# Windowed attention and MLP on one core: seven block products for group 1, and the inverse deviation as exp(-ln/2) on ScalarE

## Chip, cores and metric

The kernel runs on one core of one Trainium2 chip. The metric is the device time of one execution in microseconds (us). Before the change the median of three runs is 313.48 us (312.97 to 314.12).

## What is computed

Sliding-window causal attention over 8 batches, 8 heads, 576 positions and head size 64, with a window of 64 keys; its output, laid out as 8 x 576 rows of 512, goes through a normalisation and a two-layer perceptron with a residual.

```python
scores = (1.0 / np.sqrt(D)) * np.matmul(q, k.transpose(0, 1, 3, 2))
rel = pos[:, None] - pos[None, :]
scores = np.where((rel >= 0) & (rel < 64), scores, -1e9)
attn = softmax(scores)                       # over the keys
x = (attn @ v).transpose(0, 2, 1, 3).reshape(B, S, H * D)
mu = mean(x); var = mean((x - mu) ** 2)      # over the 512 columns
xn = (x - mu) / np.sqrt(var + 1e-06) * g_ln
out = x + np.maximum(xn @ w_ch1, 0.0) @ w_ch2   # 512 -> 2048 -> 512
```

## The kernel before

The 4608 rows are cut into nine groups of 512 rows: group g < 8 is the first 512 positions of batch g, and group 8 gathers the last 64 positions of all eight batches (the tails). A group is four blocks of 128 rows (kb 0 to 3). The outer loop runs over the groups. Its pass g, called period g here, runs the perceptron of group g and, between its pieces, the attention of batch g + 1 and the loads, casts and transposes of batch g + 2; tail blocks are done in periods 3, 5 and 7.

The order on every engine is written out by hand. mlp_units gives a list of units, and at(i, f, ...) puts a piece of other work into the slot behind unit i. Engines take their instructions in that order and wait for each other by semaphores.

- First layer: 16 units l1(hc) (line 392), each four matmuls of 512 columns into a PSUM tile hps, followed by a Relu on ScalarE into hrT (line 396). For group 1 the units are l1_half (line 513), 256 tokens of two hidden chunks at a time, so that the first half can start when two blocks of zT are there. The tiles hps, hph, ch, pA and pB come from one pool of two PSUM buffers, ps_mm.
- Second layer: groups 0 and 1 use plain products, l2 (line 404) and l2_two (line 528), each ending in add_out, which scales by rstd (from newton, lines 364 to 381, on VectorE), adds x and stores. Groups 2 to 8 use seven products of half-size blocks (line 464, unit stage(n, p)), with sums of hrT made on VectorE by s_sums (line 443), sums of W2 by w2_sums (line 561), and additions by post (line 471).
- Attention of a block j: s_mm (scores, line 283, and two Exps on ScalarE, line 290), s_mask (VectorE, line 297) and b_step (attn times v, line 317, then on VectorE reciprocal, scaling, and the row statistics mvg, lines 320 to 328).
- z_step makes the normalised rows z. In groups 0 and 1 it only subtracts the mean, on VectorE (line 338), and the factor rstd comes in at add_out. In the other groups POOL computes the factor with a power of -0.5 and then z (lines 342 to 345). A tile rsz holds the small values.
- zt_step brings z into zT: by PE transposes and a copy on ScalarE (lines 357 and 360), or for groups 2 to 7 by a DMA transpose on SP's queue (line 353), except block 3 of groups 3 and 5.
- t_main transposes q and k into qkT, by PE and a copy on ScalarE or VectorE (line 212 or 214), or by a DMA transpose; vB_cur and vB_prev copy pieces of v.

Of the kernel before, what the change touches and what calls it, by code (L numbers as in the profile page):

```python
# [10 lines left out]
FP32 = mybir.dt.float32  # L11
# [4 lines left out]
ALU = mybir.AluOpType  # L16
# [4 lines left out]
def kernel(  # L21
# [44 lines left out]
    gT = p_const.tile([128, NKC], FP32, tag="gT", name="gT")  # L66
    mhalf = p_const.tile([128, 1], FP32, tag="mhalf", name="mhalf")
    w1g = p_const.tile([128, NKC, HID], FP16, tag="w1g", name="w1g")
# [230 lines left out]
    def b_step(g, kb):  # L299
        kblk = f"{g}_{kb}"  # L300
        sfx, nb = ("r", 2) if g == NGRP - 1 else ("", None)
        if kb % 2 == 0:
            if (g, kb // 2) not in x_norm:
                for h in ((1, 0) if g // 2 == 2 else (0, 1)):
                    x_norm[(g, h)] = p_xn.tile([128, 2, DM], FP32, tag="xn" + sfx, name=f"xn_{g}_{h}", bufs=nb)
# [22 lines left out]
        nc.vector.bn_aggr(out=mvg[g][:, kb, :], in_=stats)  # L328
        if g < 2:
            z_step(g, kb)  # L330

    def z_step(g, kb):
        z = p_blk.tile([128, DM], FP16, tag="z", name=f"z_{g}_{kb}")
        zsd[(g, kb)] = z
        xv = x_norm[(g, kb // 2)][:, kb % 2, :]
        mu, var = mvg[g][:, kb, 0:1], mvg[g][:, kb, 1:2]
        if g < 2:
            nc.vector.tensor_scalar(out=z, in0=xv, scalar1=mu, scalar2=None, op0=ALU.subtract)
            return
        t = p_blk.tile([128, 3], FP32, tag="rsz", name=f"rsz_{g}_{kb}")  # L340
        ve, rs, nm = (t[:, i:i + 1] for i in range(3))
        nc.gpsimd.tensor_scalar(out=ve, in0=var, scalar1=1.0, scalar2=EPS, op0=ALU.mult, op1=ALU.add)  # L342
        nc.gpsimd.tensor_tensor(out=rs, in0=ve, in1=mhalf, op=ALU.pow)
        nc.gpsimd.tensor_scalar(out=nm, in0=mu, scalar1=rs, scalar2=-1.0, op0=ALU.mult, op1=ALU.mult)
        nc.gpsimd.tensor_scalar(out=z, in0=xv, scalar1=rs, scalar2=nm, op0=ALU.mult, op1=ALU.add)  # L345

# [36 lines left out]
    def mlp_units(g, split=0, two=False, seven=True):  # L383
# [27 lines left out]
        def add_out(kb):  # L411
            xv = x_norm[(g, kb // 2)][:, kb % 2, :]
            if g < 2:
                nc.vector.scalar_tensor_tensor(
                    out=xv, in0=ch[kb], scalar=rstd[g][:, kb:kb + 1], in1=xv, op0=ALU.mult, op1=ALU.add,
                )
            else:
                nc.vector.tensor_tensor(out=xv, in0=ch[kb], in1=xv, op=ALU.add)
            store(kb)
# [156 lines left out]
    nc.vector.memset(ones1, 1.0)  # L576
    nc.vector.memset(mhalf, -0.5)
    nc.gpsimd.affine_select(
# [87 lines left out]
    for g in range(NGRP):  # L666
        units, s_sums = mlp_units(g, (8, 16)[g] if g < 2 else 0, g == 0, g > 1)
        slots = [[] for _ in range(len(units) + 1)]
# [5 lines left out]
        if g == 0:  # L674
# [13 lines left out]
            at(17, s_mask, 1, 1)  # L688
            at(18, b_step, 1, 0)
            at(21, b_step, 1, 1)  # L690
            at(22, zt_step, 1, 0)
            at(24, zt_step, 1, 1)
            at(26, t_main, 1, 0, 1, 0)
# [10 lines left out]
        if g == 1:  # L704
            at(0, cast_qk, 2, 0)
            at(0, cast_qk, 2, 1)
            at(1, b_step, 1, 3)
            at(2, zt_step, 1, 2)
            at(13, newton, 1, 0, 4)
            at(5, zt_step, 1, 3)  # L710
            at(4, alloc_v, 2)
# [4 lines left out]
            at(4, t_main, 2, 0, 0)  # L716
            at(4, t_main, 2, 1, 0)
            at(6, t_main, 2, 0, 1)
            at(6, t_main, 2, 1, 1)
            at(25, w2_sums, 3, 0, 4)  # L720
            at(28, w2_sums, 3, 4, 8)
            for j in range(4):
                at((9, 13, 16, 19)[j], s_mm, 2, j)
                at((10, 14, 17, 20)[j], s_mask, 2, j)
                at((13, 17, 20, 23)[j], b_step, 2, j)
                at((13, 17, 20, 23)[j], z_step, 2, j)
                at((18, 21, 24, 27)[j], zt_step, 2, j)
# [10 lines left out]
            at(17, make_vB, 3)  # L738
            at(31, s_mm, 3, 0)
            at(31, s_mask, 3, 0)  # L740
            for i, (x, half) in zip((12, 24, 12, 28), ((0, 0), (1, 0), (0, 1), (1, 1))):
                at(i, t_main, 3, x, half, 0)
            at(40, load_qk, 4, 0)
            at(40, load_qk, 4, 1)
            at(40, load_v, 4, 0, 4)
        if g == 2:
            for m, i in enumerate((2, 1, 4)):
                at(4 + 2 * m, w2_sums, i, 0, 4)
                at(5 + 2 * m, w2_sums, i, 4, 8)
        if g > 1 and g + 2 < B:  # L750
# [7 lines left out]
        if g > 1 and b < B:  # L758
            for j in range(4):
# [3 lines left out]
                at((2, 7, 12, 17)[j], b_step, b, j)  # L763
                at((2, 7, 12, 17)[j], z_step, b, j)
                at((12, 12, 18, 23 if b in (3, 5) else 22)[j], zt_step, b, j)
        for n, i in enumerate(TAILS.get(g, ())):
# [3 lines left out]
            at(ts[2], b_step, NGRP - 1, i)  # L770
            at(ts[2], z_step, NGRP - 1, i)
            at(ts[3], zt_step, NGRP - 1, i)
# [34 lines left out]
        for i, u in enumerate(units):  # L807
            if g > 1 and i == 20:
                tbank["shared"] = True
            u()  # L810
            for f, a in slots[i]:
                f(*a)
# [30 lines left out]
```

The softmax here doesn't subtract the row's maximum and nothing guards it: scores larger than these inputs give would overflow.

## Time and profile before

| | |
|---|---|
| median of three runs | 313.48 us |
| the profiled execution | 314.71 us, span from first to last instruction 313.0 us |
| mean granted TensorE clock | 0.999 |
| PE matmul busy | 298.9 us (95%), 3041 matmuls |
| VectorE (DVE) busy | 205.2 us (66%) |
| ScalarE (ACT) busy | 153.4 us (49%), 258 instructions |
| GpSimd (POOL) busy | 166.3 us (53%) |
| chain of waits that ended last | PE 74%, DMA 10%, DVE 7%, SP's queue 4%, POOL 2%, ACT 1% |

A row of the groups of instructions reads: source line, engine, operation, output<-input by the program's names, shapes and count, then busy time in us and mean ns of one, then the idle time of the engine just before them with what ended most of it. A table of stages gives for each stretch of the span its length and the busy time of each engine. In a timeline each row has its start and its duration in us, and in brackets the idle time before it with its releaser. Busy time of a pipelined engine is an upper mark of its work.

### The profile page before, as it was taken

How to read it: one execution, taken by the hardware profiler on the slowest of the kernel's cores; microseconds unless marked ns; L12 is line 12 of the kernel's file. 1: busy time of each engine (PE TensorE's matmuls, PEld its weight loads, DVE VectorE, ACT ScalarE, POOL GpSimd, SP SyncE). 2: the span in 40 equal slices, each digit the busy share in tenths (PEclk: the TensorE clock that was granted, in tenths of full speed). 3: DMA queues.
4: the chain of work that ended last, by engine and by line, in shares of the span. 5: the costliest groups of instructions: out<-in, count | busy, mean ns of one | idle time of the engine just before them, and what ended most of it. 6: DMA issues, size and time to landing. Idle time of an engine off the chain costs nothing.

```text
span 313.0 us, 7473 instructions
## 1 busy us (share of the span) xinstructions
PE 298.9 (95%) x3041; PEld 194.1 (62%) x3041; DVE 205.2 (66%) x385; ACT 153.4 (49%) x258; POOL 166.3 (53%) x251
## 2 busy tenths in 40 slices
PE   6988998899999999999999999999999999999992
PEld 4457544497554468646964686459646855784582
DVE  1689585855674996589666965896669636751642
ACT  1496633477416752776247526762475058306500
POOL 7578666454760798369814983698145506200000
PEclk9999999999999999999999999999999999999999
DMA  8999999998866996798179997993690393003013
GB/s 192 267 390 290 320 336 272 280 304 184 159 144 196 268 206 105 243 312 147 37 212 316 203 149 219 316 142 67 209 172 19 62 209 117 2 2 134 0 36 101
DMA packets 109892, 57.42 MB, mean 183 GB/s; under 512 B 79841, under 2 KB 100833, under 8 KB 109858
## 3 DMA queue, kind: packets, MB, share of 16 engines
q1 hardware_dynamic: 108944, 54.02, 69.1%
q0 software_dynamic: 768, 2.80, 3.7%
q8 instruction: 24, 0.39, 0.5%
q10 hardware_dynamic: 146, 0.13, 0.1%
q14 instruction: 10, 0.08, 0.1%
HBM read 38.80 MB, written 9.44 MB: 154 GB/s over the span
## 4 chain that ended last, share of the span: by engine, by line
PE 74%; DMA 10%; DVE 7%; SPq 4%; POOL 2%; ACT 1%; issue 1%; POOLq 0%; ACTq 0%
PE hps L392 30%; PE pA L464 11%; PE pC L464 7%; PE pB L464 7%; PE ch L404 6%; DMA w2s<-in_moe_w_ch_dram 4%; DMA qk<-in_k_dram 4%; PE xps L317 3%; PE sc L283 3%; PE hph L513 3%; PE tp L226 2%; SPq L141 2%; DVE sS L443 2%; DMA w1s<-in_moe_w_ch_dram 2%; SPq L89 1%; DVE pt L297 1%
## 5 line engine op out<-in xcount | busy, mean ns | idle before, releaser
L392 PE MATMUL hps<-zT,w1g 128*128 128x512 f16 x480 | 110.4, 379 | 0.0
L396 ACT ACTIVATE hrT<-hps 128x512 f16<-128x512 f32 x120 | 71.9, 599 | 50.7 <-PE hps L392 47.2
L392 PEld LDWEIGHTS <-w1g 128*128 128x128 f16 x480 | 44.6, 98 | 49.3 <-issue 1.0
L290 ACT ACTIVATE pt<-sc 128x512 f16<-128x512 f32 x72 | 39.0, 595 | 29.8 <-DVE xn L471 15.6
L464 PEld LDWEIGHTS <-sS 128*128 128x128 f16 x448 | 43.3, 98 | 5.1
L342 POOL TENSOR_SCALAR rsz<-mvg 128x1 f32<-128x1 f32 x28 | 10.7, 382 | 60.4 <-DVE mvg L328 59.8
L128 POOL CAST qk<-qk 128x1024 f16<-128x1024 f32 x32 | 35.1, 1112 | 13.4 <-DMA qk<-in_q_dram 6.9
L464 PEld LDWEIGHTS <-hrT 128*128 128x128 f16 x336 | 32.6, 98 | 5.2
L212 ACT COPY qkT<-tp 128x1024 f16<-128x1024 f16 x16 | 16.1, 1012 | 35.2 <-PE tp L226 26.1
L297 DVE TENSOR_TENSOR pt<-pt,mask 128x1024 f16<-128x1024 f16 x32 | 25.4, 800 | 11.9 <-ACT pt L290 11.9
L471 DVE TENSOR_TENSOR xn<-pA,xn 128x512 f32<-128x512 f32 x28 | 19.2, 686 | 21.1 <-PE pA L464 21.1
L443 DVE TENSOR_TENSOR sS<-hrT 128x512 f16<-128x512 f16 (+1 forms) x42 | 24.8, 591 | 10.2 <-ACT hrT L396 10.2
L464 PE MATMUL pA<-wT,sS 128*128 128x256 f16 x224 | 26.9, 273 | 0.0
L345 POOL TENSOR_SCALAR z<-xn,rsz 128x512 f16<-128x512 f32 x28 | 25.3, 902 | 2.9
L464 PE MATMUL pC<-w2s,sS 128*128 128x256 f16 x224 | 26.8, 273 | 0.0
L325 DVE BATCH_NORM_STATS2 stats<-xn 128x6 f32<-128x512 f32 x36 | 25.0, 695 | 1.2
L323 DVE TENSOR_TENSOR xn<-xps,rcp 128x512 f32<-128x512 f32 x36 | 24.9, 692 | 1.2
L513 PE MATMUL hph<-zT,w1g 128*128 128x256 f16 x192 | 23.2, 272 | 2.3 <-ACT zT L360 1.1
L320 DVE RECIPROCAL rcp<-xps 128x8 f32<-128x8 f32 x36 | 7.4, 205 | 26.8 <-PE xps L317 26.8
L404 PE MATMUL ch<-w2s,hrT 128*128 128x512 f16 x96 | 23.1, 380 | 0.0
L513 PEld LDWEIGHTS <-w1g 128*128 128x128 f16 x192 | 18.3, 98 | 5.1 <-issue 2.6
L317 PEld LDWEIGHTS <-pt 128*64 128x64 f16 x576 | 12.2, 110 | 14.4 <-issue 6.4
(85 smaller groups left out, 395.1 us busy)
## 6 DMA issues: line engine op xcount, KB each, us to landing
out_dram<-xn SPq DMA_DIRECT2D x34, 256.0 KB, 2.6
qk<-in_q_dram SPq DMA_DIRECT2D x16, 512.0 KB, 6.2
qk<-in_k_dram SPq DMA_DIRECT2D x16, 512.0 KB, 7.4
v<-in_v_dram SPq DMA_DIRECT2D x32, 256.0 KB, 6.5
w2s<-in_moe_w_ch_dram SPq DMA_DIRECT2D x12, 512.0 KB, 5.7
w1s<-in_moe_w_ch_dram SPq DMA_DIRECT2D x4, 512.0 KB, 6.7
tk<-in_k_dram SPq DMA_DIRECT2D x8, 256.0 KB, 4.7
tv<-in_v_dram SPq DMA_DIRECT2D x8, 256.0 KB, 5.3
```

The source lines that it names most:

```text
L128: nc.gpsimd.tensor_copy(out=dst[:, :].rearrange("p (a j) e d -> p a e j d", j=j), in_=t[:, :].rearrange("p (a e j d) -> p a e j d", e=2, j ...
L290: nc.scalar.activation(out=o, in_=i, func=AF.Exp, bias=0.0, scale=scale)
L297: nc.vector.tensor_tensor(out=ptv, in0=ptv, in1=mb, op=ALU.mult)
L323: nc.vector.tensor_tensor(out=xn, in0=xps[:, :, 0:D], in1=rcp_b, op=ALU.mult)
L325: nc.vector.bn_stats(out=stats, in_=xv)
L345: nc.gpsimd.tensor_scalar(out=z, in0=xv, scalar1=rs, scalar2=nm, op0=ALU.mult, op1=ALU.add)
L392: nc.tensor.matmul(out=hps, lhsT=w1g[:, kc, 128 * hc:128 * (hc + 1)], rhs=zT[g][:, kc, :], start=(kc == 0), stop=(kc == NKC - 1),)
L396: nc.scalar.activation(out=hrT[:, hc, :], in_=hps, func=AF.Relu, bias=0.0, scale=1.0)
L404: nc.tensor.matmul(out=ch[kb], lhsT=hrT[:, hc, 128 * kb:128 * (kb + 1)], rhs=w2s[:, hc, :], start=(hc == 0), stop=(hc == NHC - 1),)
L443: nc.vector.tensor_tensor(out=o, in0=x, in1=y, op=op)
L464: nc.tensor.matmul(out=bank[which][:, p, :], lhsT=a[:, c, 128 * p:128 * p + 128], rhs=wv[:, c, :], start=(first and p == 0 and c == 0), st ...
L513: nc.tensor.matmul(out=hps[:, e], lhsT=w1g[:, kc, 128 * hc:128 * (hc + 1)], rhs=zT[g][:, kc, 256 * half:256 * half + 256], start=(kc == 0) ...
```

## The change

Group 1 joins the groups that use seven block products. For this its z must already be scaled, so newton, its rstd and the scaled add_out are left to group 0. In z_step the power on POOL is replaced, for all groups but 0, by two activations on ScalarE: lv = Ln(var + eps) and rs = Exp(-0.5 lv). z = (x - mu) * rs follows in one instruction, on VectorE for group 1 and on POOL for the others. z_step now stands three slots behind b_step in most places (two or three in periods 0 and 1). The sums of W2 move from periods 1 and 2 to the end of period 0 and the start of period 1; sums of hrT are added for group 1 in period 1. In period 1 the copies of k's transposes of batch 2 go to ScalarE (last argument 0 of t_main). Some slots of batch 3's transposes and scores move by two or three, and the tiles x_norm of groups 3, 4 and 7 are taken in reversed order (before: groups 4 and 5).

```diff
@@ -64,7 +64,7 @@
     mbias = p_const.tile([128, 64], FP16, tag="mbias", name="mbias")
     magt = p_const.tile([128, 4], FP32, tag="magt", name="magt")
     gT = p_const.tile([128, NKC], FP32, tag="gT", name="gT")
-    mhalf = p_const.tile([128, 1], FP32, tag="mhalf", name="mhalf")
+    epst = p_const.tile([128, 1], FP32, tag="epst", name="epst")
     w1g = p_const.tile([128, NKC, HID], FP16, tag="w1g", name="w1g")
     w2s = p_const.tile([128, NHC, DM], FP16, tag="w2s", name="w2s")
     w2v = w2s[:, :, :].rearrange("p (c e) (f d) -> p c e f d", e=2, f=2)
@@ -301,7 +301,7 @@
         sfx, nb = ("r", 2) if g == NGRP - 1 else ("", None)
         if kb % 2 == 0:
             if (g, kb // 2) not in x_norm:
-                for h in ((1, 0) if g // 2 == 2 else (0, 1)):
+                for h in ((1, 0) if g in (3, 4, 7) else (0, 1)):
                     x_norm[(g, h)] = p_xn.tile([128, 2, DM], FP32, tag="xn" + sfx, name=f"xn_{g}_{h}", bufs=nb)
         xv = x_norm[(g, kb // 2)][:, kb % 2, :]
         xn = xv.rearrange("p (h d) -> p h d", h=H)
@@ -326,7 +326,7 @@
         if g not in mvg:
             mvg[g] = p_grp.tile([128, 4, 2], FP32, tag="mvg" + sfx, name=f"mvg_{g}", bufs=1 if sfx else 2)
         nc.vector.bn_aggr(out=mvg[g][:, kb, :], in_=stats)
-        if g < 2:
+        if g == 0:
             z_step(g, kb)
 
     def z_step(g, kb):
@@ -334,15 +334,15 @@
         zsd[(g, kb)] = z
         xv = x_norm[(g, kb // 2)][:, kb % 2, :]
         mu, var = mvg[g][:, kb, 0:1], mvg[g][:, kb, 1:2]
-        if g < 2:
+        if g == 0:
             nc.vector.tensor_scalar(out=z, in0=xv, scalar1=mu, scalar2=None, op0=ALU.subtract)
             return
-        t = p_blk.tile([128, 3], FP32, tag="rsz", name=f"rsz_{g}_{kb}")
-        ve, rs, nm = (t[:, i:i + 1] for i in range(3))
-        nc.gpsimd.tensor_scalar(out=ve, in0=var, scalar1=1.0, scalar2=EPS, op0=ALU.mult, op1=ALU.add)
-        nc.gpsimd.tensor_tensor(out=rs, in0=ve, in1=mhalf, op=ALU.pow)
-        nc.gpsimd.tensor_scalar(out=nm, in0=mu, scalar1=rs, scalar2=-1.0, op0=ALU.mult, op1=ALU.mult)
-        nc.gpsimd.tensor_scalar(out=z, in0=xv, scalar1=rs, scalar2=nm, op0=ALU.mult, op1=ALU.add)
+        t = p_blk.tile([128, 2], FP32, tag="rsz", name=f"rsz_{g}_{kb}")
+        lv, rs = t[:, 0:1], t[:, 1:2]
+        nc.scalar.activation(out=lv, in_=var, func=AF.Ln, bias=epst[:, 0:1], scale=1.0)
+        nc.scalar.activation(out=rs, in_=lv, func=AF.Exp, bias=0.0, scale=-0.5)
+        eng = nc.vector if g == 1 else nc.gpsimd
+        eng.tensor_scalar(out=z, in0=xv, scalar1=mu, scalar2=rs, op0=ALU.subtract, op1=ALU.mult)
 
     def zt_step(g, kb, eng="act"):
         z = zsd.pop((g, kb))
@@ -410,7 +410,7 @@
 
         def add_out(kb):
             xv = x_norm[(g, kb // 2)][:, kb % 2, :]
-            if g < 2:
+            if g == 0:
                 nc.vector.scalar_tensor_tensor(
                     out=xv, in0=ch[kb], scalar=rstd[g][:, kb:kb + 1], in1=xv, op0=ALU.mult, op1=ALU.add,
                 )
@@ -574,7 +574,7 @@
     nc.vector.memset(mask, 1.0)
     nc.vector.memset(magt, RSQRT_MAGIC)
     nc.vector.memset(ones1, 1.0)
-    nc.vector.memset(mhalf, -0.5)
+    nc.vector.memset(epst, EPS)
     nc.gpsimd.affine_select(
         out=mask[0:64], in_=mask[0:64], compare_op=ALU.is_gt, fill=0.0,
         base=0, channel_multiplier=1, pattern=[[-1, 64]],
@@ -664,7 +664,7 @@
 
     TAILS = {3: [0], 5: [1], 7: [2, 3]}
     for g in range(NGRP):
-        units, s_sums = mlp_units(g, (8, 16)[g] if g < 2 else 0, g == 0, g > 1)
+        units, s_sums = mlp_units(g, (8, 16)[g] if g < 2 else 0, g == 0, g > 0)
         slots = [[] for _ in range(len(units) + 1)]
 
         def at(i, f, *a):
@@ -687,9 +687,14 @@
             at(17, s_mm, 1, 1)
             at(17, s_mask, 1, 1)
             at(18, b_step, 1, 0)
+            at(20, z_step, 1, 0)
             at(21, b_step, 1, 1)
-            at(22, zt_step, 1, 0)
-            at(24, zt_step, 1, 1)
+            at(23, z_step, 1, 1)
+            at(23, zt_step, 1, 0)
+            at(26, zt_step, 1, 1)
+            for m, i in enumerate((3, 2, 4)):
+                at(25 + 2 * m, w2_sums, i, 0, 4)
+                at(26 + 2 * m, w2_sums, i, 4, 8)
             at(26, t_main, 1, 0, 1, 0)
             at(27, t_main, 1, 1, 1, 1)
             at(28, vB_cur, 1, 2, 0)
@@ -703,27 +708,31 @@
             at(31, b_step, 1, 2)
         if g == 1:
             at(0, cast_qk, 2, 0)
-            at(0, cast_qk, 2, 1)
+            at(2, cast_qk, 2, 1)
             at(1, b_step, 1, 3)
-            at(2, zt_step, 1, 2)
-            at(13, newton, 1, 0, 4)
-            at(5, zt_step, 1, 3)
+            at(1, z_step, 1, 2)
+            at(4, z_step, 1, 3)
+            at(2, w2_sums, 1, 0, 4)
+            at(3, w2_sums, 1, 4, 8)
+            at(3, zt_step, 1, 2)
+            at(7, zt_step, 1, 3)
+            for i in range(1, 5):
+                at((12, 12, 13, 14)[i - 1], s_sums, 0, 4, i)
+                at((16, 16, 18, 20)[i - 1], s_sums, 4, 8, i)
             at(4, alloc_v, 2)
             at(4, alloc_qkT, 2)
             at(4, alloc_vB, 2)
             at(5, cast_v, 2, 0, 4)
             at(5, make_vB, 2)
             at(4, t_main, 2, 0, 0)
-            at(4, t_main, 2, 1, 0)
+            at(4, t_main, 2, 1, 0, 0)
             at(6, t_main, 2, 0, 1)
-            at(6, t_main, 2, 1, 1)
-            at(25, w2_sums, 3, 0, 4)
-            at(28, w2_sums, 3, 4, 8)
+            at(6, t_main, 2, 1, 1, 0)
             for j in range(4):
                 at((9, 13, 16, 19)[j], s_mm, 2, j)
                 at((10, 14, 17, 20)[j], s_mask, 2, j)
                 at((13, 17, 20, 23)[j], b_step, 2, j)
-                at((13, 17, 20, 23)[j], z_step, 2, j)
+                at((15, 19, 22, 25)[j], z_step, 2, j)
                 at((18, 21, 24, 27)[j], zt_step, 2, j)
             at(3, load_qk, 3, 0)
             at(4, load_qk, 3, 1)
@@ -736,17 +745,13 @@
             at(14, cast_v, 3, 2, 4)
             at(17, alloc_vB, 3)
             at(17, make_vB, 3)
-            at(31, s_mm, 3, 0)
-            at(31, s_mask, 3, 0)
-            for i, (x, half) in zip((12, 24, 12, 28), ((0, 0), (1, 0), (0, 1), (1, 1))):
+            at(28, s_mm, 3, 0)
+            at(29, s_mask, 3, 0)
+            for i, (x, half) in zip((12, 22, 12, 25), ((0, 0), (1, 0), (0, 1), (1, 1))):
                 at(i, t_main, 3, x, half, 0)
             at(40, load_qk, 4, 0)
             at(40, load_qk, 4, 1)
             at(40, load_v, 4, 0, 4)
-        if g == 2:
-            for m, i in enumerate((2, 1, 4)):
-                at(4 + 2 * m, w2_sums, i, 0, 4)
-                at(5 + 2 * m, w2_sums, i, 4, 8)
         if g > 1 and g + 2 < B:
             at(11, alloc_qkT, g + 2)
             if g + 2 >= XQ:
@@ -761,14 +766,14 @@
                     at((2, 7, 12)[j - 1], s_mm, b, j)
                     at((3, 8, 13)[j - 1], s_mask, b, j)
                 at((2, 7, 12, 17)[j], b_step, b, j)
-                at((2, 7, 12, 17)[j], z_step, b, j)
+                at((5, 10, 15, 20)[j], z_step, b, j)
                 at((12, 12, 18, 23 if b in (3, 5) else 22)[j], zt_step, b, j)
         for n, i in enumerate(TAILS.get(g, ())):
             ts = (10, 11, 14, 20) if n else (1, 2, 5, 11)
             at(ts[0], s_mm, NGRP - 1, i)
             at(ts[1], s_mask, NGRP - 1, i)
             at(ts[2], b_step, NGRP - 1, i)
-            at(ts[2], z_step, NGRP - 1, i)
+            at(ts[2] + 3, z_step, NGRP - 1, i)
             at(ts[3], zt_step, NGRP - 1, i)
         n = g + 2
         if g > 1 and n < B:
@@ -805,7 +810,7 @@
             at(7, t_tail, TAILS[g][1], 0)
             at(8, t_tail, TAILS[g][1], 1)
         for i, u in enumerate(units):
-            if g > 1 and i == 20:
+            if g > 0 and i == 20:
                 tbank["shared"] = True
             u()
             for f, a in slots[i]:
```

## The prediction

> **What bounds the kernel now.** I read the page's busy shares first, then the groups of instructions, then a table of stages cut at the borders of period 2, then ScalarE's timeline there.
>
> ```profile
> PE 298.9 (95%) x3041; PEld 194.1 (62%) x3041; DVE 205.2 (66%) x385; ACT 153.4 (49%) x258; POOL 166.3 (53%) x251
> ...
> L392 PE MATMUL hps<-zT,w1g 128*128 128x512 f16 x480 | 110.4, 379 | 0.0
> L396 ACT ACTIVATE hrT<-hps 128x512 f16<-128x512 f32 x120 | 71.9, 599 | 50.7 <-PE hps L392 47.2
> ...
> L342 POOL TENSOR_SCALAR rsz<-mvg 128x1 f32<-128x1 f32 x28 | 10.7, 382 | 60.4 <-DVE mvg L328 59.8
> ```
>
> TensorE (PE) is busy in 95% of the span. ScalarE's Relus wait for PE and never the reverse (the hps row has no idle time), and POOL's small operations wait for their input, so POOL has time to spare.
>
> ```profile
> 96.40:112.80 16.40, 16.40 (x169) 7.93 (x162) 13.80 (x27) 12.93 (x23) 9.27 (x11) 1.00 0.95 240
> 112.80:128.50 15.70, 15.30 (x177) 13.04 (x175) 12.20 (x21) 4.77 (x7) 13.71 (x21) 1.00 0.93 156
> ```
>
> Columns: stretch, length, then busy time of PE, PEld, DVE, ACT, POOL. The first stretch is the first layer of period 2, the second its second layer. ScalarE's 49% hides two things: it is busy 12.9 of 16.4 us in the first layer, and 4.8 of 15.7 us in the second. The first-layer stages are where an addition to ScalarE meets a limit.
>
> ```profile
> 103.56 0.60 ACT L396 ACTIVATE hrT<-hps 128x512 f16<-128x512 f32 x1 [0.27 <-PE hps L392]
> 104.42 0.60 ACT L396 ACTIVATE hrT<-hps 128x512 f16<-128x512 f32 x1 [0.27 <-PE hps L392]
> 105.13 1.08 ACT L290 ACTIVATE pt<-sc 128x512 f16<-128x512 f32 x2
> 106.11 0.60 ACT L396 ACTIVATE hrT<-hps 128x512 f16<-128x512 f32 x1
> ```
>
> A unit of PE takes 0.86 us, its Relu 0.60; ScalarE idles 0.27 per unit, and at an attention step (b_step and s_mm, 0.73 on PE; two Exps, 1.0 on ScalarE) not at all. The hps tiles have two PSUM buffers, so PE can be only two units ahead.
>
> ```profile
> 1.35 1.28 ACT L212 ACT_TABLE_LOAD   x1 [1.35 <-PEq L827]
> ```
>
> That is the only activation table load of the whole kernel.
>
> **What the Trainium skill says.** "ScalarE: Activation LUTs", section "What ACT_TABLE_LOAD costs": a switch of the table set is an instruction on ScalarE of about 1283 ns, plus about 1380 ns of drain. The trace has 1.28 us for the load; 5.37 us of waiting for PE follow it, so no drain can be seen or excluded. Section "Table sets: the hidden batching unit": Relu and copy are in every set, and one set holds both exp and ln. The program as built does not use that one throughout: it has 65 loads where the one before has 1, one ahead of every Ln and one ahead of every Exp of z_step. The Relus and attention's Exps need no more. "TensorE: Matmul & The Clock Gate", "Part 1": PE falls to half clock after an idle window of about 3.4 us; the trace shows 1.00 granted in both stretches above, with PE never idle that long.
>
> **The change, part by part.**
>
> (1) *Inverse deviation on ScalarE.* All blocks but group 0's (32) drop three POOL operations (about 0.54, 0.55 and 0.26 us in the timeline; POOL is not on the path: gain 0 on PE) and put on ScalarE's queue: load, Ln, load, Exp. The trace has no 128x1 activation; the skill's section above prices 280 ns with a pointer bias, 186 ns with an immediate, plus 0.83 ns an element. By the same formula 128x512 is 613 ns; the trace has 599, near enough. So T = 1.28 + 0.28 + 1.28 + 0.19 = 3.03 us, with dispatch **T = 3.1** (estimate). Bounds: below, 0.47 if neither load costs anything; above, 3.1 + 2 x 1.38 = 5.8 with the drains. I take 3.1: the built program issues no drain of its own. The first load also waits for mvg (DVE); z_step was moved three slots behind b_step, so in first layers mvg is there (101.5 for a block due at 103.3).
>
> What is queued behind: the next Relus. Step it at slot 5 of period 2. Let Relu 5 end at 0. Units 6 and 7 end at 0.92 on PE, then slot 7's attention step, 1.65. Unit 8 needs Relu 6, which now ends at T + 0.60: it starts at T + 0.67 = 3.77, 2.1 us late. Then Relu 7 and two Exps precede Relu 8, which ends at T + 2.8; unit 10 could start at T + 2.4: 0.5 more. About 0.1 of that is lost without the block. So **T - 0.6 = 2.5 us of PE per block in a first layer**. PE regains nothing later, since it had no idle time to give.
>
> Which blocks fall there, by ScalarE's order in the changed program: two each in periods 2, 4 and 6, three in 3 and 5 (a tail block too), one in 7: 13 x 2.5 = **32.5**.
>
> (2) *Second layers of periods 2 to 7.* ScalarE has about 11 us free there, so kb 2's block (3.1) is covered. kb 3's mvg comes at 119.4 in period 2; the block ends at 122.5, then the waiting qkT copy (1.0) and POOL's z (0.9): 123.5, where PE wants to transpose z at 121.9: 1.7 late, in periods 2 and 4. In 3, 5 and 6 z goes by a DMA transpose (median 3.0 us to landing): period 3's z would be ready at 155.7, its zT at 158.7, with the next first layer at 160.1: covered by 1.4; I allow 1.0 in all for its queue. In period 7 the tail's mvg is at 269.85, z at 273.9, PE's transpose at 273.1: 0.8. Sum **5.2**.
>
> (3) *Period 0.* Before, DVE needs nobody for z. Now z_0 waits for ScalarE and stands in DVE's queue ahead of b_step (1,1) and of add_out(0): mvg 44.5, z_0 at 47.7 instead of 44.6, second mvg 50.1 instead of 47.4, add_out(0) done at 50.9 instead of 49.2, which frees the PSUM bank of ch_2; then z_1 at 53.3 and ztp of kb 1 at 53.9 (49.0 before, but now due two units later). Behind it DVE has the six W2 sums (0.66 each, up to 1.29 for two), a qkT copy (1.23) and the masks of the last two score blocks. Following DVE's order, add_out(3) ends near 65.5 instead of 62.3, and period 1's third unit waits for that bank: **+3.1**.
>
> (4) *Period 1, first layer.* Blocks kb 2 and 3 stand between its Relus, and two qkT copies (1.0 each) move from DVE to ScalarE. Stepped: third Relu 69.9 (63.5 + 6.4), fifth 71.8, second block to 74.9, two copies to 76.9, Relu 5 and 6 to 78.1, two copies to 80.1, Relu 7, zT copy to 81.3. The second half of the tokens starts at 81.4 against 69.85: 11.5, of which **8.4** are new. SP and POOL's moved cast (slot 0 to 2) have landed data and free time: 0.
>
> (5) *Period 1, rest.* Seven products replace 64 matmuls of 512 columns (3.45 us per 16) by 112 of 256 (1.75 per 16): 13.8 - 12.25 = 1.5 gained on PE. newton's 0.6 us wait goes. The eight sums of hrT (0.69 each) on DVE replace newton (3.0) and two copies (2.5): 0. Against that, four blocks of 3.1, two pairs of Exps and two copies (2.0), 17 us, stand in a stage of 16: the sc buffers, a masked block and the second qkT transpose wait about 2.0 together, and kb 3's rs comes at the very end, so that z (0.9) and its DMA transpose (3.0) reach zT about 3.3 late. Net 5.3 - 2.1 = **+3.2**. Bounds: -2.1 and +8.
>
> The eight W2 sums leave periods 1 and 2, where DVE has time: 0. x_norm's tiles of three groups are taken in another order because group 1 now stores rows 256 to 511 first: the tile asked for first is the one freed first, 0; covered by the stores' 2.6 us to landing.
>
> Sum: 32.5 + 5.2 + 3.1 + 8.4 + 3.2 = **52.4 us**. The profiled execution took 314.71 (span 313.0); the median of the three runs is 313.48, 1.2 below. So 367.1 against its own time, **366** against the median. Each 0.1 us in T is worth about 2.5 us (13 first-layer blocks, about 4 in later second layers, 8 in the serial chains of periods 0 and 1).
>
> **Rivals.**
> A. *Each load drains* (T = 5.8): 2.7 x 25 = 68 more, **433**, and PE's gaps would pass 3.4 us, so the clock could fall too. For it: the skill's figure. Against: no drain is among the instructions. One drain per pair gives 400. Chance 0.12.
> B. *The stalls overlap more than I step*: blocks in periods 0 and 1 run in slack that my chain denies, and half of the first-layer stalls fall in PE's own waits: about half of the sum, **340**. The absence of idle time on PE speaks against. Chance 0.09.
> C. *The loads are no real switch* (no time for them, because exp and ln lie in one set): T = 0.47, below the 0.6 that the two buffers cover. Only the 1.5 and 0.6 of (5) remain, less latency in period 0: **312**. It decides from T under 0.6. Against: the built program loads anew at every turn, and one load showed 1.28 us. Chance 0.04.
> D. My forecast, 350 to 380: chance 0.75.
>
> **How the numbers follow.** About 0.5% (1.6 us) is what a measurement of this kernel can tell from no change. A, B and D lie far above that; C splits 0.03 faster, 0.01 within. The range 345 to 400 leaves out the upper part of A (0.09) and the lower parts of B and C (0.09).
>
> **What would show it.** Right: 65 ACT_TABLE_LOADs, ScalarE's busy time up by some 95 us to near 250; in the first layers PE waiting for "ACT hrT L396" twice a period for about 2 us, where no such wait stands now; first-layer stages of some 21.4 us in place of 16.4, and second layers near 16; POOL's L342 to L344 rows gone. Wrong: one load only (C), gaps of over 1 us after each load (A), PE still over 90% busy, or a span under 345.

## The result and the profile after

The changed kernel takes 378.98 us in the median of four runs (375.49 to 381.11), the kernel before 313.62 us on the same chip (four runs, 312.97 to 314.12). The ratio is 1.2075, 95% interval 1.1976 to 1.2173. The profiled execution took 379.96 us, its span is 378.2 us (before 313.0), and the mean granted clock is 0.954 (before 0.999).

From the page of the kernel after, the busy shares and then rows of the groups of instructions:

```profile
PE 319.5 (84%) x3089; PEld 205.4 (54%) x3089; DVE 212.9 (56%) x383; ACT 247.6 (65%) x388; POOL 156.9 (41%) x167
...
L392 PE MATMUL hps<-zT,w1g 128*128 128x512 f16 x480 | 119.5, 398 | 23.2 <-ACT hrT L396 19.3
...
L345 POOL TENSOR_SCALAR z<-xn,mvg,rsz 128x512 f16<-128x512 f32 x28 | 58.2, 2078 | 138.8 <-ACT rsz L343 84.1
...
L342 ACT ACT_TABLE_LOAD x32 | 41.1, 1283 | 7.9 <-DVE mvg L328 7.5
...
L343 ACT ACT_TABLE_LOAD x32 | 41.1, 1283 | 0.6
```

PE is busy in 84% of its span instead of 95%. The hps row had no idle time; now it has 23.2 us, 19.3 of them behind ScalarE's Relu. There are 64 table loads of 1.283 us in z_step, 82.2 us together. One row changed that the prediction gave no weight to: POOL's z takes 2078 ns in the mean.

ScalarE's timeline in period 2, at the place where a block stands between two Relus:

```profile
118.72 0.60 ACT L396 ACTIVATE hrT<-hps 128x512 f16<-128x512 f32 x1 [0.27 <-PE hps L392]
119.33 1.28 ACT L342 ACT_TABLE_LOAD   x1
120.62 0.29 ACT L342 ACTIVATE rsz<-mvg,epst 128x1 f32<-128x1 f32 x1
120.94 1.28 ACT L343 ACT_TABLE_LOAD   x1
122.23 0.20 ACT L343 ACTIVATE rsz<-rsz 128x1 f32<-128x1 f32 x1
122.34 1.06 ACT L396 ACTIVATE hrT<-hps 128x512 f16<-128x512 f32 x2
```

From the first load's start to the end of Exp it is 3.10 us, and no idle time lies between the five instructions. The table of stages for period 2 (stretch, length, then busy time of PE, PEld, DVE, ACT and POOL, PEclk, DMA share, GB/s):

```profile
110.80:133.00 22.20, 18.36 (x160) 8.48 (x161) 10.41 (x20) 17.34 (x29) 5.21 (x4) 0.92 1.00 226
133.00:153.10 20.10, 17.03 (x177) 13.87 (x176) 11.80 (x21) 10.67 (x15) 13.93 (x16) 0.92 0.35 82
```

The first layer takes 22.2 us instead of 16.4, the second 20.1 instead of 15.7. Both have a granted clock of 0.92. PE's longest waits (what it waited for, us in total, times, longest):

```profile
PE hps L392 <- ACT hrT L396: 19.3, 11, 2.6
PE ztp L357 <- POOL z L345: 6.8, 3, 2.3
PE hps L392 <- DMA zT<-z: 3.4, 2, 2.7
```

The first is what the prediction named. The second is where it was short. The third it had forecast at the border of period 2, where zT was to be about 3.3 us late; the wait there is 2.74 us.

### The profile page after: what moved, and what is told of

Its sections match the earlier page's. It is cut to its first block, busy times and chain, and to the rows that moved or that the text cites. A ratio compares the mean times of both kernels' runs of the same rounds, so it can differ in the third digit from the quotient of the medians.

```text
span 378.2 us, 7630 instructions
## 1 busy us (share of the span) xinstructions
PE 319.5 (84%) x3089; PEld 205.4 (54%) x3089; DVE 212.9 (56%) x383; ACT 247.6 (65%) x388; POOL 156.9 (41%) x167
## 4 chain that ended last, share of the span: by engine, by line
PE 28%; ACT 20%; DVE 13%; issue 12%; DMA 11%; POOL 7%; SPq 5%; POOLq 1%; ACTq 0%; DVEq 0%
PE hps L392 14%; ACT L342 6%; DVE sS L443 5%; ACT L343 4%; PE pA L464 4%; DMA qk<-in_q_dram 3%; POOL z L345 3%; ACT hrT L396 3%; SPq L141 3%; PE pC L464 2%; PE pB L464 2%; PE hph L513 2%; DMA vB<-vA 2%; ACT pt L290 2%; DVE pt L297 2%
## 5 line engine op out<-in xcount | busy, mean ns | idle before, releaser
L392 PE MATMUL hps<-zT,w1g 128*128 128x512 f16 x480 | 119.5, 398 | 23.2 <-ACT hrT L396 19.3
L345 POOL TENSOR_SCALAR z<-xn,mvg,rsz 128x512 f16<-128x512 f32 x28 | 58.2, 2078 | 138.8 <-ACT rsz L343 84.1
L392 PEld LDWEIGHTS <-w1g 128*128 128x128 f16 x480 | 47.0, 101 | 78.7 <-issue 34.4
L464 PEld LDWEIGHTS <-sS 128*128 128x128 f16 x512 | 51.0, 101 | 7.5
L342 ACT ACT_TABLE_LOAD x32 | 41.1, 1283 | 7.9 <-DVE mvg L328 7.5
L464 PEld LDWEIGHTS <-hrT 128*128 128x128 f16 x384 | 38.0, 100 | 6.9 <-issue 0.5
L343 ACT ACT_TABLE_LOAD x32 | 41.1, 1283 | 0.6
L471 DVE TENSOR_TENSOR xn<-pA,xn 128x512 f32<-128x512 f32 x32 | 21.9, 685 | 34.1 <-PE pA L464 34.1
L443 DVE TENSOR_TENSOR sS<-hrT 128x512 f16<-128x512 f16 (+1 forms) x46 | 29.8, 647 | 12.7 <-ACT hrT L396 11.7
L464 PE MATMUL pA<-wT,sS 128*128 128x256 f16 x256 | 33.9, 289 | 0.1
L464 PE MATMUL pC<-w2s,sS 128*128 128x256 f16 x256 | 31.5, 276 | 0.0
L513 PEld LDWEIGHTS <-w1g 128*128 128x128 f16 x192 | 19.4, 104 | 7.1 <-issue 3.6
L518 ACT ACTIVATE hrT<-hph 128x512 f16<-128x512 f32 x24 | 14.2, 600 | 12.2 <-PE hph L513 12.1
```

The costliest lines, as they stand in the source:

```text
L342: nc.scalar.activation(out=lv, in_=var, func=AF.Ln, bias=epst[:, 0:1], scale=1.0)
L343: nc.scalar.activation(out=rs, in_=lv, func=AF.Exp, bias=0.0, scale=-0.5)
L345: eng.tensor_scalar(out=z, in0=xv, scalar1=mu, scalar2=rs, op0=ALU.subtract, op1=ALU.mult)
L392: nc.tensor.matmul(out=hps, lhsT=w1g[:, kc, 128 * hc:128 * (hc + 1)], rhs=zT[g][:, kc, :], start=(kc == 0), stop=(kc == NKC - 1),)
L443: nc.vector.tensor_tensor(out=o, in0=x, in1=y, op=op)
L464: nc.tensor.matmul(out=bank[which][:, p, :], lhsT=a[:, c, 128 * p:128 * p + 128], rhs=wv[:, c, :], start=(first and p == 0 and c == 0), st ...
```

## Experiments

The kernels are shown in one table: how much later than before period 2 starts (terms 3 to 5 of the sum), and by how much the six first layers (term 1) and the six second layers (term 2) of periods 2 to 7 are longer than before, read on PE in the one profiled execution of each, in us, to about 0.1. The ratio is that of all timed runs to the kernel before on the same chip. e3's profiled execution was its lowest run (323.62), e10's its highest (324.03). e9 has one run, 317.45 us, and serves for durations on POOL only.

| kernel | start of period 2 | first layers | second layers | median | ratio (95%) |
|---|---|---|---|---|---|
| forecast | +14.7 | +32.5 | +5.2 | 366 | |
| after | +14.4 | +34.6 | +16.3 | 378.98 | 1.2075 (1.1976 to 1.2173) |
| e1 one load in all | +8.5 | +5.2 | +3.6 | 330.35 | 1.0532 (1.0493 to 1.0570) |
| e2 POOL's old form of z | +10.5 | +31.6 | +3.9 | 361.49 | 1.1551 (1.1502 to 1.1601) |
| e3 both | +5.8 | +3.7 | -0.8 | 327.50 | 1.0406 (1.0366 to 1.0446) |
| e8 e3, loads in first layers | +7.4 | +34.2 | -0.8 | 355.15 | 1.1299 (1.1264 to 1.1335) |
| e4 power on POOL again | +13.1 | +0.1 | -0.9 | 327.80 | 1.0462 (1.0422 to 1.0502) |
| e6 after, more matmuls | +14.4 | +34.4 | +14.7 | 378.02 | 1.2063 (1.2023 to 1.2102) |
| e10 e3, slots moved | +5.9 | +3.7 | -0.3 | 322.40 | 1.0262 (1.0231 to 1.0293) |
| e11 e10 without the sums | -0.4 | +3.7 | -0.7 | 317.54 | 1.0127 (1.0099 to 1.0155) |
| e5 inverse deviation alone | -0.9 | +3.7 | +0.1 | 317.84 | 1.0136 (1.0109 to 1.0162) |
| e7 the same with the loads | +1.4 | +32.2 | +3.4 | 350.42 | 1.1173 (1.1134 to 1.1212) |
| e12 e5, tails two slots later | -1.8 | +0.2 | +1.1 | 315.76 | 1.0049 (1.0030 to 1.0069) |

### What the loads cost: e1, e7 and e5, e8

e1 puts one load of the set that holds Ln, Exp and Relu ahead of everything, after which the program has no other:

```diff
+    nc.scalar.add_instruction(mybir.InstLoadActFuncSet(
+        name=nc.get_next_instruction_name(), ins=[], outs=[], act_func_set_id=6))
     load_qk(0, 0)
```

> The changed kernel with one line ahead of everything: an explicit load of the table set that holds exp, ln, relu and copy. All 64 later loads fall away; Ln, Exp and their order stay. Theory 1 (the loads are nearly the whole cost): each block on ScalarE shrinks from 3.10 us to about 0.5, below the 0.6 that two PSUM buffers cover; 310 to 314 us, no waits of PE for hrT in first layers. Theory 2 (a large part comes from z on POOL, 2.07 us now against 0.8 before, and from the slots that moved): it stays well above the kernel before, 320 to 330. Theory 3 (the clock falls in PE's gaps): the gaps go with the loads, so it cannot be told from theory 1 here; granted clock back at 0.99 or more.

It takes 330.35 us, 48.6 less than after. ScalarE's timeline in period 2 of e1:

```profile
112.56 0.60 ACT L396 ACTIVATE hrT<-hps 128x512 f16<-128x512 f32 x1 [0.27 <-PE hps L392]
113.06 0.29 ACT L342 ACTIVATE rsz<-mvg,epst 128x1 f32<-128x1 f32 x1
113.37 0.20 ACT L343 ACTIVATE rsz<-rsz 128x1 f32<-128x1 f32 x1
113.48 0.58 ACT L396 ACTIVATE hrT<-hps 128x512 f16<-128x512 f32 x1
```

The block is now 0.5 us long and PE does not wait for it. So one set does serve all three functions, as the Trainium skill says ("ScalarE: Activation LUTs", "Table sets: the hidden batching unit"); the program as built only did not use it. Yet 330 us is not the 312 of rival C: something else costs 17 us.

The pair e5 and e7 is the kernel before with Ln and Exp for groups 2 to 8 and the later z slots, group 1 as it was; e5 has the one load, e7 has 57.

```diff
-        nc.gpsimd.tensor_scalar(out=ve, in0=var, scalar1=1.0, scalar2=EPS, op0=ALU.mult, op1=ALU.add)
-        nc.gpsimd.tensor_tensor(out=rs, in0=ve, in1=mhalf, op=ALU.pow)
+        nc.scalar.activation(out=lv, in_=var, func=AF.Ln, bias=epst[:, 0:1], scale=1.0)
+        nc.scalar.activation(out=rs, in_=lv, func=AF.Exp, bias=0.0, scale=-0.5)
...
-                at((2, 7, 12, 17)[j], z_step, b, j)
+                at((5, 10, 15, 20)[j], z_step, b, j)
...
-            at(ts[2], z_step, NGRP - 1, i)
+            at(ts[2] + 3, z_step, NGRP - 1, i)
```

> The kernel before with only the inverse deviation changed: Ln and Exp on ScalarE for groups 2 to 8, z_step two or three slots later as in the change, one table set loaded at the start, POOL's z in its old form; group 1 keeps plain products and newton. If what the changed kernel loses besides loads and form lies in periods 0 and 1 (period 1's VectorE), only the tail blocks' later z is left, 1.8 us each in periods 3 and 5: 315 to 318. If moving the power off POOL gains anything: under 313.

> The same, without the explicit load, so that 56 table loads come in ahead of Ln and Exp: the loads' price on the otherwise unchanged kernel. By the rule of 2.5 us for each of 13 blocks in first layers, 1 to 2 us in second layers of periods 2 and 4, 1 in 7, and some 2 in period 1: 38 to 42 us more than without them, 353 to 359.

The 56 further loads cost 32.6 us, less than the 38 to 42 expected, and most of it in the first layers (+32.2 against +3.7). e8 shows that it is the loads there and not the place of the functions: e3 with two loads of the same set put back into the 13 blocks that the prediction counted.

```diff
+        first = (3 <= g <= 7 and kb < 2) or (g == NGRP - 1 and kb < 3)
+        if first:
+            nc.scalar.add_instruction(mybir.InstLoadActFuncSet(
+                name=nc.get_next_instruction_name(), ins=[], outs=[], act_func_set_id=6))
         nc.scalar.activation(out=lv, in_=var, func=AF.Ln, ...)
...
```

> As the run with one set and POOL's old form, but with two table loads (of the same set again) put back into just the 13 blocks that stand between the Relus of a first layer in periods 2 to 7. The rule of the prediction, T - 0.6 a block with T = 3.1, gives 13 x 2.5 = 32.5 us more than without them. If a block's cost is really spread over later waits: under 26 more; if it also delays what follows: 36 or more.

27.7 us more by the medians, 30.5 in the first layers of the profiled executions: 2.1 to 2.35 us per block, where the prediction had 2.5. Part of this is not the block itself but a lowered clock (see e6).

### POOL's form of z: e2, e3, e9

The change also rewrote z on POOL, from x*rs + nm to (x - mu)*rs. The trace's view of that tile, first after, then before (minimum, median and maximum in ns):

```profile
L345 POOL TENSOR_SCALAR z<-xn,mvg,rsz x28: 2059/2072/2266, 93.8 to 334.5; 128x512 f16<-128x512 f32 x28
```

```profile
L345 POOL TENSOR_SCALAR z<-xn,rsz x28: 762/795/1611, 80.6 to 271.5; 128x512 f16<-128x512 f32 x28
```

e2 is the kernel after with the old form; e3 is e2 with e1's single load.

```diff
-        eng.tensor_scalar(out=z, in0=xv, scalar1=mu, scalar2=rs, op0=ALU.subtract, op1=ALU.mult)
+        if g == 1:
+            nc.vector.tensor_scalar(out=z, in0=xv, scalar1=mu, scalar2=rs, op0=ALU.subtract, op1=ALU.mult)
+            return
...
+        nc.gpsimd.tensor_scalar(out=nm, in0=mu, scalar1=rs, scalar2=-1.0, op0=ALU.mult, op1=ALU.mult)
+        nc.gpsimd.tensor_scalar(out=z, in0=xv, scalar1=rs, scalar2=nm, op0=ALU.mult, op1=ALU.add)
```

> The changed kernel, loads and all, but POOL makes z in its old form, x * rs + (-mu * rs), with one small product ahead, instead of (x - mu) * rs. Theory 1: no more than 2 us less than the changed kernel. Theory 2: z is ready about 1.0 us earlier (2.07 against 0.3 + 0.8), which shortens PE's waits for z in the second layers of periods 2, 4 and 7 and for zT at the borders: 3 to 8 us less, 371 to 376. Theory 3: as theory 2, plus fewer second layers at a lowered clock.

> One table set loaded at the start, and POOL's z in its old form: both suspects gone, the seven products, W2 sums and moved slots of the change stay. If loads and form add up in separate places, the run with one set (330.3) loses about 9 us of its second layers in periods 2 to 7, which then last as before: 319 to 323. If they share one wait, 326 or more. If all the rest of the change costs nothing: 312 to 314.

With the loads in place the old form saves 17.5 us, where 3 to 8 were expected; 12.4 of them are in the second layers (+3.9 instead of +16.3), and some of those are the clock's (below). Without the loads it saves 2.9 (330.35 to 327.5). So the slow form is dear only where z is late already.

e9 is the kernel before with four forms of z, one for each kb, seven instructions each: kb 0 (x - mu)*rs, kb 1 (x + (-mu))*rs, kb 2 x*rs - mu*rs, kb 3 x*rs + (-mu*rs).

> The kernel before, with POOL's z made in four forms by block: kb 0 (x - mu) * rs, kb 1 (x + (-mu)) * rs, kb 2 x * rs - mu * rs, kb 3 as before x * rs + (-mu * rs). If the order of the operations (multiply, then add) is what is fast: kb 0 and 1 at 2.0 us and kb 2 and 3 at 0.8. If only the pair multiply-add has a fast path: kb 3 alone at 0.8. If subtract is slow: kb 0 and 2 at 2.0. If it is contention and not the form: all alike.

Its groups of instructions on POOL (lines 345, 348, 351, 354 are kb 0 to 3; busy us, mean ns, idle before):

```profile
L345 POOL TENSOR_SCALAR z<-xn,mvg,rsz 128x512 f16<-128x512 f32 x7 | 15.7, 2236 | 0.8
L351 POOL TENSOR_SCALAR z<-xn,rsz 128x512 f16<-128x512 f32 x7 | 15.3, 2193 | 0.7
...
L348 POOL TENSOR_SCALAR z<-xn,rsz 128x512 f16<-128x512 f32 x7 | 9.3, 1322 | 0.7
...
L354 POOL TENSOR_SCALAR z<-xn,rsz 128x512 f16<-128x512 f32 x7 | 5.9, 840 | 0.8 <-DMA zT<-z 0.2
```

The two forms with a subtraction never took less than 2077 ns; both with additions went down to 762 to 767 ns. It is the subtraction, in either place, and not the order of the two steps. Why is not shown. Additions were at times slow as well (up to 2127 ns), so a single duration on POOL does not tell the form.

### Does the lowered clock cost something: e6

In the kernel after, units 7 and 12 of the first layers of periods 2 to 6 do their matmuls three times, 17 us of work for PE where it waits.

```diff
-            for kc in range(NKC):
+            for kc in list(range(NKC)) * (3 if 2 <= g <= 6 and hc in (7, 12) else 1):
```

> The changed kernel with the matmuls of first-layer units 7 and 12 made three times over in periods 2 to 6 (same tile, the last pass counts): 1.7 us of PE work in front of the place where PE waits 1.85 to 2.6 us for ScalarE, twice a period, 17 us of added matmul work in all. Theory 1: the added work hides in the waits, and the time stays within 3 us of the changed kernel. Theory 3: the gaps no longer let the clock fall in first layers, granted clock 0.97 to 0.98, and 4 to 10 us less. If the waits were not real: 17 us more.

The time is 378.02 us against 378.98: within the 3 us of the first theory, without the 4 to 10 us of the third. PE's wait for hrT falls to the second line of this list of waits, and the mean clock rises from 0.954 to 0.973:

```profile
PE ztp L357 <- POOL z L345: 8.1, 5, 2.3
PE hps L392 <- ACT hrT L396: 5.1, 2, 2.6
```

Seventeen us of PE's work cost nothing in all: most of them fit into PE's waits for ScalarE. But that the total stayed does not show that the clock costs nothing, because the stages moved in opposite ways. The first layer of period 4, first after, then e6 (columns as in the table of stages above):

```profile
192.10:214.40 22.30, 18.29 (x162) 8.49 (x161) 11.28 (x22) 17.34 (x29) 5.44 (x5) 0.92 1.06 259
```

```profile
192.50:213.00 20.50, 20.13 (x179) 9.53 (x177) 11.23 (x22) 17.35 (x29) 5.33 (x4) 1.00 1.06 263
```

Here e6 has 16 more matmuls, 3.4 us of work at full clock, and is 1.8 us shorter, at a clock of 1.00 in place of 0.92. Period 6 shows the same. In periods 3 and 5 the stage became 0.6 us longer, and in period 7, where e6 adds no work, 2.3 us, with a lowered clock (0.93) and two new waits for POOL. This took back what the clock had brought. Two rows of PE in after, from the first layers of periods 2 and 4, show the clock itself:

```profile
122.97 4.70 PE L392 MATMUL hps<-zT,w1g 128*128 128x512 f16 x20 [1.85 <-ACT hrT L396]
```

```profile
202.90 6.16 PE L392 MATMUL hps<-zT,w1g 128*128 128x512 f16 x20 [1.85 <-ACT hrT L396]
```

The same 20 matmuls after the same wait take 4.70 and 6.16 us. The granted clock is 1.00 around the first row and 0.50 for 3.4 us (203.6 to 207.0) in the second. e7 has the same pair in periods 6 and 4 of one execution: 4.70 and 6.16 us after waits of 1.85, and stages of 20.5 and 22.0 us with the same two blocks in each. So a lowered clock costs some 1.5 us there, on top of what a block on ScalarE takes. In a second layer it is alike. PE in the second layer of period 2, first after, then e2:

```profile
144.88 0.40 PE L357 MATMUL ztp<-ident,z 128*128 128x128 f16 x4 [2.26 <-POOL z L345]
145.12 3.20 PE L464 MATMUL pA<-wT,sS 128*128 128x256 f16 x16
148.11 2.33 PE L464 MATMUL pB<-wT,hrT 128*128 128x256 f16 x16
```

```profile
137.78 0.40 PE L361 MATMUL ztp<-ident,z 128*128 128x128 f16 x4 [1.76 <-POOL z L349]
138.01 1.91 PE L468 MATMUL pA<-wT,sS 128*128 128x256 f16 x16
139.76 1.91 PE L468 MATMUL pB<-wT,hrT 128*128 128x256 f16 x16
```

There a POOL instruction that is 1.3 us longer made the wait 0.5 longer and the products behind it 1.7 longer. The length of the wait alone does not decide whether the clock falls. In period 4 a wait of 2.33 us stands in after and in e6. First after, then e6:

```profile
226.27 0.40 PE L357 MATMUL ztp<-ident,z 128*128 128x128 f16 x4 [2.33 <-POOL z L345]
226.51 2.70 PE L464 MATMUL pA<-wT,sS 128*128 128x256 f16 x16
229.00 2.84 PE L464 MATMUL pB<-wT,hrT 128*128 128x256 f16 x16
```

```profile
224.83 0.40 PE L357 MATMUL ztp<-ident,z 128*128 128x128 f16 x4 [2.33 <-POOL z L345]
225.07 1.91 PE L464 MATMUL pA<-wT,sS 128*128 128x256 f16 x16
226.81 1.91 PE L464 MATMUL pB<-wT,hrT 128*128 128x256 f16 x16
```

What else decides it was not found.

### Periods 0 and 1: e4, e10, e11

e4 is the kernel after with the power on POOL for groups 1 to 8 and the old form, no Ln and no Exp; group 1 keeps its seven products and its z on VectorE.

```diff
-        nc.scalar.activation(out=lv, in_=var, func=AF.Ln, bias=epst[:, 0:1], scale=1.0)
-        nc.scalar.activation(out=rs, in_=lv, func=AF.Exp, bias=0.0, scale=-0.5)
+        nc.gpsimd.tensor_scalar(out=ve, in0=var, scalar1=1.0, scalar2=EPS, op0=ALU.mult, op1=ALU.add)
+        nc.gpsimd.tensor_tensor(out=rs, in0=ve, in1=mhalf, op=ALU.pow)
...
```

> The changed kernel with z_step's inverse deviation as it was (power of -0.5 on POOL, for group 1 too, whose z stays on VectorE); seven products, the W2 sums in period 0 and all moved slots stay. Theories 1 and 3: 310 to 314 us, near the run with one table set; the seven products' 1.5 us and newton's 0.6 may show. If the moved work of period 0 and the qkT copies on ScalarE cost something by themselves: 315 to 325.

327.80 us is more than either expectation. First and second layers are back at the old lengths (+0.1 and -0.9), so all their growth came from z_step. Period 2 still starts 13.1 us late, now because of another wait, the first in PE's list:

```profile
PE ztp L360 <- DVE z L345: 6.8, 2, 6.3
```

With the power on POOL, group 1's z in period 0 stands behind POOL's casts: they run to 52.5 us, and the z follows at 53.4. The granted clock is 0.50 in the 10.2 us from 49.6 on. That is a reason for ScalarE in this place, if its tables stay.

e10 is e3 with the W2 sums in slots 8 to 11 of period 1, k's copies of batch 2 on VectorE again, and the last zt_step of group 2 one slot earlier, ahead of two stores on SP's queue.

```diff
-            for m, i in enumerate((3, 2, 4)):
-                at(25 + 2 * m, w2_sums, i, 0, 4)
-                at(26 + 2 * m, w2_sums, i, 4, 8)
...
+            for m, i in enumerate((3, 2, 4, 1)):
+                at(8 + m, w2_sums, i, 0, 4)
+                at(8 + m, w2_sums, i, 4, 8)
...
-                at((18, 21, 24, 27)[j], zt_step, 2, j)
+                at((18, 21, 24, 26)[j], zt_step, 2, j)
...
-            at(4, t_main, 2, 1, 0, 0)
+            at(4, t_main, 2, 1, 0)
...
```

> As the run with one set and POOL's old form, with three slots changed: the W2 sums move from the end of period 0 into period 1's first layer (VectorE idles there for some 9 us at a stretch), batch 2's k copies go back to VectorE, and zt of group 2's last block is issued one unit earlier, ahead of group 1's first two stores on SP's queue. If the W2 sums and the store order are what is left of the loss: 2.3 us for the wait for zT at the border and 3 to 5 us in periods 0 and 1, down to 311 to 315. If the loss comes from seven products themselves: no change against the run that it is based on.

322.4 us, against 327.5 for e3 and 311 to 315 expected. The 5.1 us are not the slots alone: four of e3's six runs took 327.2 to 328.0 at a clock of 0.985 to 0.991, the other two 323.6 and 324.4 at 0.996 and 0.997, and all of e10's had 0.998 or more. Against those two the gain is 1.6 us. The wait for the DMA transpose at the border of period 2 (2.3 us in e3) is gone; the period still starts 5.9 us late, because PE's waits for masks grew from 3.1 us in e3 to 6.1. PE's longest line of waits from 38 to 103 us (total, times, longest), and VectorE's timeline:

```profile
PE xps L317 <- DVE pt L297: 6.1, 4, 2.8
```

```profile
70.37 4.62 DVE L565 TENSOR_TENSOR wT<-w2s 128x1024 f16<-128x1024 f16 x2
74.91 2.12 DVE L565 TENSOR_TENSOR wT<-wT,w2s 128x1024 f16<-128x1024 f16 x2
76.96 1.28 DVE L565 TENSOR_TENSOR wT<-w2s,wT 128x1024 f16<-128x1024 f16 x2
78.16 0.68 DVE L297 TENSOR_TENSOR pt<-pt,mask 128x1024 f16<-128x1024 f16 x1
```

A mask of 0.68 us stands behind six W2 sums, the first two of which take 4.62 us, where the prediction priced two at 1.29 at most; PE waits 1.7 us for this mask. e11 leaves out all W2 sums and group 1's sums of hrT; its products read W2 and hrT in their place, as many matmuls as before, so its output is another.

> The run with the three slots changed (322.4), with the eight W2 sums and group 1's eight sums of hrT left out (the products read W2 and hrT themselves, so the values are others, and the matmuls as many). If VectorE's queue is what keeps period 1 long (masks waiting behind sums): periods 0 and 1 fall by 6 to 8 us, 314 to 317. If it is the products, the order of stores or the moved transposes: 320 or more.

317.54 us, 4.9 less than e10 (4.2 by the ratios), and period 2 starts at 96.0 (before 96.4). So the sums cost 4 to 5 us where e10 has them. In after, where six of the W2 sums stand in period 0, PE's waits for masks are only 1.9 us from 38 to 111 us; what the sums cost there is not known, since no run leaves them out of after itself. The gain of the seven products is there on PE: PE is busy 13.75 us with the products of period 1's second layer in after and e3, 13.76 in e11, and 15.17 before, 1.4 us less, where 1.5 was forecast. But in after and e3 waits take more than that back, and in e11 period 2 starts only 0.4 us earlier than before, less than the 0.9 by which e5 and e12, alike up to there, differ at the same border.

### The rest: e12

e3, e5, e10 and e11 have the same 3.7 us too many in the first layers of periods 3 and 5. In e5 a tail block's z is waited for twice:

```profile
PE ztp L357 <- POOL z L345: 3.3, 2, 1.6
```

z_step of a tail was moved three slots later and its zt_step was not. e12 is e5 with that moved too.

```diff
-            at(ts[3], zt_step, NGRP - 1, i)
+            at(ts[3] + 2, zt_step, NGRP - 1, i)
```

> The kernel before with the inverse deviation as exp(-ln/2) for groups 2 to 8, one table load in all, and a tail block's zt_step two slots later (13, and 22 for the second tail of period 7) than in e5_inverse_alone, which took 317.84 us. Theory: what is left of e5 above the kernel before (4.4 us) is mostly PE's wait for POOL's z of the tail block in periods 3 and 5 (1.6 us each), because z_step was moved three slots later and zt_step stayed; with two slots more the two waits go and the time is 313.5 to 315. Rival: the 4 us are spread (second layers, the end), and the two waits only turn into waits at the next z: 317 to 318.5, no change.

The growth of the first layers falls to 0.2, and the time to 315.76 us, 1.0049 of before (e5 1.0136): most of it, not all, and just above the range expected. No version here beats the kernel before.

## Why the prediction was right, and where it was off

The mechanism and its place were right: table loads on ScalarE ahead of the next Relus, with PE waiting. The size was nearly right, 366 forecast and 379 measured, inside the range, and in the stretch of case D (350 to 380) by 1 us; but two of the three parts of the sum came out near in part by luck.

- **(1) First layers: the sum nearly right, with two errors that cancel.** T was taken as 3.1 us and is 3.10. The rule T - 0.6 gave 2.5 us for each of 13 blocks, 32.5; the stages grew by 34.6. A block alone costs less: at a clock of 1.00 the first layers of period 2 in e2 and of period 6 in e7, with two blocks each, are 4.2 us longer than before, so 2.1 for a block and some 27 for 13. The lowered clock, which the sum put at nothing, adds, by the difference from these 4.2 us, 1.7 to 1.8 in each of periods 2, 4 and 6 of after (5.2). Most of the rest lies in period 7, where PE also waits 2.5 us for a copy of tkT on ScalarE.
- **(2) Second layers: mis-sized**, 5.2 against 16.3. The step put POOL's z at 0.9 us, the old row's duration, though the instruction was rewritten, and called the loss of three POOL operations a gain of 0. POOL's z became 1.3 us longer at the one place where POOL is on the path: behind a late rs and ahead of PE's transpose. With the old form (e2) the term is 3.9. Of the 12.4 us between, the lowered clock in periods 2, 4 and 7 has some 4.9 (the transpose and the products behind it take 5.5, 5.5 and 4.4 us instead of 3.8, 3.8 and 2.85); PE's waits for POOL's z are 3.2 longer (6.8 against 3.6), and 3.0 are waits for casts of qk on POOL, of which e2 has almost none.
- **(3) to (5) Periods 0 and 1: near in sum**, 14.4 against 14.7, and at two stations: period 1's third unit at 65.10 (forecast 65.5), the second half of the tokens at 79.93 (forecast 81.4). Not every wait behind this is the one named. Period 1 starts 3.3 us late, and PE's longest wait just before it is 1.72 us for a mask on VectorE; at the third unit itself PE has no wait for add_out(3). The clock is 0.50 for 3.4 us from 70.5 and from 80.7, which was put at nothing. At the border of period 2 zT is late, as forecast, but because of POOL's z of 2.07 us:

```profile
106.02 2.07 POOL L345 TENSOR_SCALAR z<-xn,mvg,rsz 128x512 f16<-128x512 f32 x1 [2.01 <-DVE xn L471]
```

```profile
108.12 1.20 SPq L353 DMA_TRANSPOSE zT<-z  x1
```

  In e3, with the old form, that z is done 2.2 us before its transpose is issued, behind two stores on SP's queue. The 1.5 us gained on PE came (1.4), and waits took them back.
- **That the clock would fall only with gaps over 3.4 us: wrong.** In after it is 0.50 from 111.4 to 114.8, behind a gap of 2.74 us, and from 203.6 to 207.0, behind one of 1.85:

```profile
203.60:207.00 3.40, 3.40 (x10) 1.19 (x9) 2.62 (x5) 1.79 (x4) 0.94 (x1) 0.50 1.09 236
```

  The Trainium skill ("TensorE: Matmul & The Clock Gate", "Part 1: The HAM clock gate") has half clock, and a window of about 3.4 us, and these stretches agree with that. That PE must first be idle for a whole window, as the same page says, they do not show: no gap of period 2 was above 2.74 us, and the measurement decides.
- **Rivals.** A (drains): there is no gap after a load, and T is 3.10, so it falls. B (overlap): the first layers grew by the whole sum. C (no real switch): true of the tables if they are loaded once, but such a kernel takes 330.35 us and not 312. C took as 0 what else the change moved: POOL's form, VectorE's sums, the tails' slots, and the clock that falls with the waits.

By the medians the 65.4 us divide so, each with the lowered clock that goes with it: 51.5 go with the loads and POOL's form together (378.98 to e3's 327.5), of which the loads take 34.0 with the old form and 48.6 with the slow one; 5.1 go from e3 to e10, only some 1.6 of it by the slots; 4.9 with the sums (e11), at e10's places. Of the 4 us left about half is the tails' slots (e12 on e5: 2.1); the other half was not traced further.

## What to carry to other kernels

Two functions that a program alternates can mean a table load each, even where one set holds both: read the loads in the built program, and place one load of the common set yourself. Price a rewritten instruction as a new one, on an idle engine too, if a late chain runs through it. A step that is moved moves its deadline with it: what reads its result must be moved by as much. And a total that does not move can hide stages that moved in opposite ways: compare stage by stage.

## What was not expected of the hardware

- POOL's tensor_scalar on 128x512 took 2059 ns or more with a subtraction (after), and from 762 ns up with additions and multiplications alone (e9).
- A load of the set that is already there costs as much as another: e8's 26 loads of one set, 1283 ns each, brought back 27.7 us.
- The granted clock fell to 0.50 for 3.4 us after waits of PE from 1.85 us up, and elsewhere, after waits of the same length, it did not: after 1.85 us it fell in period 4 of after and not in period 2, after 2.33 us in period 4 of after and not of e6. Where it fell among the 20 matmuls of a first layer, they took 6.16 us instead of 4.70.
- Two sums of 128x1024 on VectorE took 4.62 us at one place and 1.28 at another of the same execution (e10); one of the first pair took 4.02 us, the other 0.68. What slowed them was not tried.
